# GpSimd's row transfers issued singly, weight splits in pairs, and the tail of attention in another order

## The chip, the core and the metric

The kernel runs on one core of one Trainium2 chip. The metric is the device time of the whole launch in microseconds (us). Five engines work side by side and in order, each on its own list of instructions: TensorE (PE; its weight loads are shown as PEld), VectorE (DVE), ScalarE (ACT), GpSimd (POOL) and SyncE (SP), which issues most transfers. They wait for one another through semaphores.

## The reference

The program is an attention layer whose output rows go through a mixture of eight experts. Cut to what is computed:

```python
# attention: 4 batches, 8 heads, 768 positions, head size 64
scores = q @ k.T / sqrt(64) + bias            # bias falls with distance, one slope per head
keep   = first 8 positions, or the 96 positions up to the row's own
a      = softmax(where(keep, scores, -1e9));  x = (a @ v), rows of 512 for 3072 tokens
# experts: 8, one per token
logits = x @ w_gate + modality_bias[modality_id]
e      = argmax(logits);  gate = softmax(logits)[e]
out[t] = gate[t] * (relu(x[t] @ w1[e]) @ w2[e])      # w1 512x1024, w2 1024x512
```

## The kernel before

**Attention.** The 3072 tokens are 24 blocks of 128 rows. `step(n)` (one per block, software pipelined) puts on TensorE the scores of block n (L235), the transposes of the probabilities of block n-1 (`pt`, L279), the product with the values of block n-2 (`pv`, L301 and L313), and the router's small products of blocks n-3 and n-4 (`gate_a`, `gate_b`, `gate_c`: `tx`, `lp`, `lq`). `xr` scales a finished block and stores its rows to `x_rows`. One batch is six blocks; after each batch `route_a` to `route_f` find every token's expert and its place in a sorted list, and `route_c` writes six times 128 entries of that list (`ids_sorted`) by an indirect transfer from GpSimd.

**Experts.** Tokens of one expert are worked off in slots, in this order: e0, e1 (512 rows each, from the first two batches), p0 (512), g0 (128), p1 (512), g1 (128), p2 (512), u0 (256). A slot of 512 rows has eight groups, one of 128 has two, and one of 256 four. A group is `l1` (twelve matmuls into `ph`; ReLU on ScalarE gives `hh`, VectorE gives the remainder `hl`) and, one group later, `l2` through `finish_group` (twelve matmuls into `po`). Every operand is split into a high and a low part, so each product takes three matmuls. Such names carry the slot: `php` and `pop` are those of a p slot, `phg` and `pog` of a g slot; `ahp`/`alp` and `bhp`/`blp` are the two parts of a p slot's first and second weights. A g slot has tokens on the other side, and transposes its hidden rows (`l1_t`).

**What a slot needs beforehand.** Its weights are loaded by SyncE in eight pieces of 512 KB into six buffers `raw`; a buffer is loaded again once its piece has been split. `split` does one piece: ScalarE rounds it (L606), VectorE subtracts (L607). Its rows are fetched from `x_rows` by GpSimd (`gather_x`, 128 rows a transfer, tile `xg`), and `x_t` transposes one such tile on TensorE (`mt`) and splits it on ScalarE and VectorE (`xh`, `xl`). The results go out by GpSimd, 128 rows a transfer (`fin`, L775). A single set of up to 32 leftover tokens (`few_x`, `few_t`, `few_l1`, `few_ht`, `few_l2`) is worked in plain fp32 beside e1 and p0; `few_l2` (L738) is 64 small matmuls straight from the raw weights.

**The order.** The order on TensorE, ScalarE and VectorE is the order in which the code is written (`manual_schedule`). In the loop over slots u and groups g, `run(k)` takes k splits from a sorted list of due ones, and `fill` issues writes and gathers and transposes the next slot's rows. GpSimd and SyncE have queues that are placed by the framework's own simulation and worked in order. `spaced(ins, x)` makes an instruction wait for instruction x.

Of the kernel before, what the change touches and what calls it, by code (L numbers as in the profile page):

```python
# [19 lines left out]
P = 128  # L20
# [6 lines left out]
NBLK = NT // P  # L27
# [37 lines left out]
def moe_attention_kernel(  # L65
# [278 lines left out]
    def gate_a(b, i):  # L344
        xv = xrs.pop((b, i))
        tx = p_t(f"tx{b}_{i}")
        for c in range(4):
            nc.tensor.transpose(tx[:, c * P : (c + 1) * P], xv[:, c * P : (c + 1) * P], ident)
# [61 lines left out]
    by = [pv_end]  # L410

# [40 lines left out]
    def route_c(b, j):  # L452
# [8 lines left out]
        if b + 1 < B:  # L461
            spaced(ins, by[0])
# [105 lines left out]
    def gather_x(s, ts, early=False):  # L568
        if 0 in ts:
            s.xg = xgp.tile([P, 4, DM], F32, tag="xg", name=f"xg{s.name}")  # L570
        for t in ts:
            ins = nc.gpsimd.indirect_dma_start(
                out=s.xg[:, t, :],
                out_offset=None,
                in_=s.xsrc,
                in_offset=bass.IndirectOffsetOnAxis(ap=s.ui[:, t, 0:1], axis=0),
            )
            if early:
                spaced(ins, pv_end)
            elif s.straight:  # L580
                spaced(ins, pe_end)
# [110 lines left out]
    def few_x(s):  # L692
        s.xg = mp.tile([M, DM], F32, tag="xgf", name="xgf")
        nc.gpsimd.indirect_dma_start(
# [4 lines left out]
        )  # L699

# [377 lines left out]
    for b in range(B):  # L1078
# [8 lines left out]
        for j in range(NB):  # L1087
            at(n0 + NB + 7 + (j // 3 if b else j), route_c, b, j)
# [95 lines left out]
    for u in range(2):  # L1184
        at(LAST + 4 + u, lambda u=u: gather_x(eslots[0], (2 * u, 2 * u + 1), True))
# [90 lines left out]
    e0.mx = mx[0]  # L1276
    x_t(e0, 0)
# [16 lines left out]
    gate_c(*gates(NBLK - 2))  # L1294
# [6 lines left out]
    def rest():  # L1301
        by[0] = pe_end
        late = [job for n in sorted(todo) for job in todo[n]]
        writes.extend(args for f, args in late if f is route_c)
        for f, args in late:
            if f is route_c:
# [113 lines left out]
    def fill(u, g):  # L1420
# [5 lines left out]
        for i in range(2):  # L1426
            if writes and (writes[0][0], "pi") in rt:
                route_c(*writes.pop(0))
        if len(order) == NE and len(slist) == NPS + NUS + NGR and not writes:

            order.extend(slist[j] for j in ORDER)
            load_on()
# [10 lines left out]
        if nx is not None:  # L1443
            nx.mx = mx[(u + 1) % 2]
            if s.nt == 4 and 3 <= g < 3 + nx.nt:
                x_t(nx, g - 3)
            elif s.nt < 4 and 2 * g + 1 < nx.nt:
                x_t(nx, 2 * g + 1)
# [159 lines left out]
```

## Time and profile before

| | before |
|---|---|
| runs shown | 465.87, 467.57, 471.68 us; median 467.57 |
| profiled execution | 465.37 us, span 463.6 us |
| TensorE | busy 432.3 us, 93% of the span; mean granted clock 0.986 |
| VectorE, ScalarE, GpSimd | 57%, 50%, 25% |
| chain that ended last | PE 82%, issue 7%, ACT 6%, DVE 3%, POOL 1% |

Attention lasts until about 140 us, then comes a tail in which the last blocks' router products and the first slot's row transposes share TensorE, and from about 156 us on the expert slots follow each other. The last row of the table is the chain of waits followed back from the end; "issue" in it is time in which the engine waited for nothing that the profile shows.

### The profile page before, as it was taken

How to read it: one execution, taken by the hardware profiler on the slowest of the kernel's cores; microseconds unless marked ns; L12 is line 12 of the kernel's file. 1: busy time of each engine (PE TensorE's matmuls, PEld its weight loads, DVE VectorE, ACT ScalarE, POOL GpSimd, SP SyncE). 2: the span in 40 equal slices, each digit the busy share in tenths (PEclk: the TensorE clock that was granted, in tenths of full speed). 3: DMA queues.
4: the chain of work that ended last, by engine and by line, in shares of the span. 5: the costliest groups of instructions: out<-in, count | busy, mean ns of one | idle time of the engine just before them, and what ended most of it. 6: DMA issues, size and time to landing. Idle time of an engine off the chain costs nothing.

```text
span 463.6 us, 11673 instructions
## 1 busy us (share of the span) xinstructions
PE 432.3 (93%) x4376; PEld 357.8 (77%) x4376; DVE 266.2 (57%) x892; ACT 232.6 (50%) x635; POOL 114.8 (25%) x243
## 2 busy tenths in 40 slices
PE   7999999999898896999999979998999987999994
PEld 6888888887777684788887758886888865888993
DVE  7887888787795473878543313356333455343540
ACT  6887788787774331435332413266333464232631
POOL 7500031157642077003500520004500050000031
PEclk9999999999998999999999989999999998999998
DMA  8999999999887152235612362248732485323121
GB/s 285 349 329 349 348 357 350 325 333 281 301 283 306 69 178 82 85 119 185 212 46 93 105 219 90 95 153 298 240 129 90 135 258 197 123 93 103 65 91 52
DMA packets 37873, 90.44 MB, mean 195 GB/s; under 512 B 6047, under 2 KB 8095, under 8 KB 37808
## 3 DMA queue, kind: packets, MB, share of 16 engines
q1 hardware_dynamic: 32848, 76.29, 49.4%
q0 software_dynamic: 4672, 12.85, 7.9%
q8 instruction: 36, 0.59, 0.6%
q10 hardware_dynamic: 288, 0.48, 0.3%
q14 instruction: 29, 0.24, 0.2%
HBM read 75.21 MB, written 14.45 MB: 193 GB/s over the span
## 4 chain that ended last, share of the span: by engine, by line
PE 82%; issue 7%; ACT 6%; DVE 3%; POOL 1%; POOLq 0%; ACTq 0%; DVEq 0%
PE pt L279 8%; PE s L235 6%; PE x L313 5%; PE php L654 5%; PE php L652 5%; PE php L653 5%; PE pop L680 4%; PE pop L681 4%; PE pop L682 4%; PE phe L652 3%; PE poe L680 3%; PE poe L682 3%; PE poe L681 3%; PE phe L654 3%; PE phe L653 3%
## 5 line engine op out<-in xcount | busy, mean ns | idle before, releaser
L265 ACT ACTIVATE pr<-sc,nmx 128x168 f32<-128x168 f32 x192 | 81.0, 424 | 20.2 <-DVE nmx L254 20.2
L656 DVE SCALAR_TENSOR_TENSOR hlp<-php,hhp 128x512 fp32r<-128x512 f32 x24 | 16.6, 692 | 81.4 <-ACT hhp L655 78.1
L254 DVE CUSTOM_DVE_ANT_0 sc<-s,tbl 128x168 f32<-128x168 f32 x192 | 50.8, 328 | 7.7 <-PE s L235 7.5
L655 ACT ACTIVATE hhp<-php 128x512 fp32r<-128x512 f32 x24 | 14.4, 598 | 78.3 <-PE php L654 78.3
L279 PE MATMUL pt<-ident,pr 128*128 128x128 f32 x288 | 45.7, 289 | 1.6 <-DVE rin L325 0.5
L288 DVE COPY pT<-pt 128x384 f32<-128x384 f32 x72 | 37.7, 549 | 15.4 <-PE pt L279 12.7
L652 PE MATMUL php<-xhp,ahp 128*128 128x512 f32 x96 | 39.2, 408 | 4.3 <-ACT ahp L606 4.3
L279 PEld LDWEIGHTS pt<-ident,pr 128*128 128x128 f32 x288 | 30.8, 143 | 13.4 <-issue 5.3
L235 PE MATMUL s<-kt,qt 64*64 64x168 f32 x768 | 38.2, 319 | 3.0 <-DVE lgt L367 1.8
L654 PE MATMUL php<-xhp,alp 128*128 128x512 f32 x96 | 38.5, 401 | 1.2 <-DVE alp L607 1.2
L653 PE MATMUL php<-xlp,ahp 128*128 128x512 f32 x96 | 38.1, 397 | 0.0
L680 PE MATMUL pop<-bhp,hhp 128*128 128x512 f32 x96 | 37.6, 391 | 0.0
L682 PE MATMUL pop<-bhp,hlp 128*128 128x512 f32 x96 | 37.4, 390 | 0.0
L681 PE MATMUL pop<-blp,hhp 128*128 128x512 f32 x96 | 37.4, 389 | 0.0
L455 POOL DMA_INDIRECT ids_sorted<-tki,pi x24 | 24.6, 1025 | 50.7 <-PE lq L366 20.1
L265 ACT ACTIVATION_READ_ACCUMULATOR pr<-sc,nmx 128x1 f32 x192 | 36.1, 188 | 0.0
L235 PEld LDWEIGHTS s<-kt,qt 64*64 64x64 f32 x768 | 27.7, 136 | 7.6 <-DVE lgt L367 2.4
L655 ACT ACTIVATE hhe<-phe 128x512 fp32r<-128x512 f32 x16 | 9.6, 598 | 46.5 <-PE phe L654 46.5
L313 PE MATMUL x<-vx,pT 128*64 128x64 f32 x768 | 28.8, 226 | 1.6 <-issue 1.5
L313 PEld LDWEIGHTS x<-vx,pT 128*64 128x64 f32 x768 | 25.0, 138 | 3.7 <-issue 2.0
L680 PE MATMUL poe<-bhe,hhe 128*128 128x512 f32 x64 | 25.1, 393 | 2.5 <-issue 2.5
L652 PE MATMUL phe<-xhe,ahe 128*128 128x512 f32 x64 | 26.0, 407 | 0.0
(378 smaller groups left out, 977.4 us busy)
## 6 DMA issues: line engine op xcount, KB each, us to landing
vx<-in_v_l SPq DMA_DIRECT2D x24, 512.0 KB
kt<-in_k_t SPq DMA_DIRECT2D x23, 464.0 KB
x_rows<-xr SPq DMA_DIRECT2D x24, 256.0 KB
qt<-in_q_t SPq DMA_DIRECT2D x23, 256.0 KB
vl<-in_v_s SPq DMA_DIRECT2D x48, 96.0 KB
rawe0a<-in_moe_w SPq DMA_DIRECT2D x4, 512.0 KB
rawe0b<-in_w SPq DMA_DIRECT2D x4, 512.0 KB
rawe1a<-in_moe_w SPq DMA_DIRECT2D x4, 512.0 KB
```

The lines of the kernel that those rows point to most:

```text
L235: nc.tensor.matmul(ps[h][64 * half : 64 * half + 64, c : c + W], qt[hs, hp, 64 * half : 64 * half + 64], kt[hs, hp, k0 : k0 + W], start=Tr ...
L254: V.tensor_tensor_reduce(out=sc, in0=pss[n, hp // 2][h][:, hp % 2 * W : (hp % 2 + 1) * W], in1=(tbl0 if n % NB == 0 else tbl)[:, hh, :], o ...
L265: last[0] = nc.scalar.activation(pr[:, h * (PRW - W) : h * (PRW - W) + W], sc, AF.Exp, bias=nmx[:, hh : hh + 1], scale=-1.0, accum_out=sum ...
L279: nc.tensor.transpose(tp[:, j * P : (j + 1) * P], pr[:, o : o + P], ident)
L288: V.tensor_copy(pT.rearrange("p a b -> p (a b)"), tp[:, 0 : 3 * P])
L313: pv_end[0] = nc.tensor.matmul(px[h][64 * half : 64 * half + 64, hp * D : (hp + 1) * D], pT[:, 2 * h, 64 * half : 64 * half + 64], vx[:, h ...
L652: nc.tensor.matmul(out_, hi, xh, start=(c == 0), stop=False)
L653: nc.tensor.matmul(out_, hi, xl, start=False, stop=False)
L654: pe_end[0] = nc.tensor.matmul(out_, lo, xh, start=False, stop=(c == 3))
L680: nc.tensor.matmul(s.po[t], hh[:, tt], hi, start=(fc == 0), stop=False)
L681: nc.tensor.matmul(s.po[t], hh[:, tt], lo, start=False, stop=False)
L682: pe_end[0] = nc.tensor.matmul(s.po[t], hl[:, tt], hi, start=False, stop=(fc == 7))
```

## The change

GpSimd's transfers: in attention, the list entries of batches two to four are written two per step instead of three, one step earlier, and within a step (as the early gathers of e0) they wait in turn for the last value product and for the last `gate_a` transpose. In the slots, `fill` only puts gathers in a list, and a new function `move` issues one gather or one write after `l1` and one after `l2`, each held until the latest matmul there; before, a whole slot's gathers were issued together, and the last batch's writes waited for no matmul.

Splits: `run` takes two per group in slots of 512 rows from e1 on (before one). In a g slot the next slot's first weights are split first, and its rows are transposed two tiles before each `l2` (before one before and one after). Tail: two router products are placed ahead of e0's transposes.

```diff
+        by[0] = tx_end if b and j % 2 else pv_end       # write_in_step(b, j), then route_c(b, j)
...
-        if b + 1 < B:
+        if (by[0] or [None])[0] is not None:
             spaced(ins, by[0])
...
-            at(n0 + NB + 7 + (j // 3 if b else j), route_c, b, j)
+            at(n0 + NB + 6 + (j // 2 if b else j), write_in_step, b, j)
...
-    for u in range(2):
-        at(LAST + 4 + u, lambda u=u: gather_x(eslots[0], (2 * u, 2 * u + 1), True))
+    for t in range(4):
+        at(LAST + 4 + t // 2, lambda t=t: gather_x(eslots[0], t, tx_end if t % 2 else pv_end))
...
+    gate_b(*gates(NBLK - 3))
+    gate_a(*gates(NBLK - 2))
     x_t(e0, 0)
     x_t(e0, 1)
     rinv(NBLK - 1)
     pv(NBLK - 1)
     sQ.close()
     mp = pool("mp")
-    gate_b(*gates(NBLK - 3))
-    gate_a(*gates(NBLK - 2))
     gate_c(*gates(NBLK - 3))
+    xr(NBLK - 1)
+    gate_b(*gates(NBLK - 2))
     x_t(e0, 2)
-    xr(NBLK - 1)
     x_t(e0, 3)
     gate_a(*gates(NBLK - 1))
-    gate_b(*gates(NBLK - 2))
+    gate_c(*gates(NBLK - 2))
...
-        for i in range(2):
-            if writes and (writes[0][0], "pi") in rt:
-                route_c(*writes.pop(0))
...
-            gather_x(order[ahead[1]], range(order[ahead[1]].nt))
+            s2 = order[ahead[1]]
+            gathers.extend((gather_x, s2, t) for t in range(s2.nt))
             if ahead[1] == NE:
-                few_x(fs[0])
+                gathers.append((few_x, fs[0]))
...
+    def move():
+        if gathers:
+            f, *args = gathers.pop(0)
+            if f is gather_x:
+                args.append(pe_end)
+            f(*args)
+        elif writes and (writes[0][0], "pi") in rt:
+            route_c(*writes.pop(0))
...
-            to_small = g + 1 == s.groups and nx is not None and nx.nt < 4
             if u or g:
-                run(2 if to_small or s.nt == 2 else 1 if s.nt == 4 else 2 * (1 - g))
-            if s.nt < 4 and nx is not None and 2 * g < nx.nt:
-                nx.mx = mx[(u + 1) % 2]
-                x_t(nx, 2 * g)
+                run((2 if u else 1) if s.nt > 1 else 2 * (1 - g))
+                move()
+            if s.nt < 4 and nx is not None:
+                for t in range(2 * g, min(2 * g + 2, nx.nt)):
+                    next_rows(u, t)
             if before:
                 finish_group(*before)
...
             if s.nt == 1 and g == 0:
                 run(2)
+            if not u or 0 < g < 7:
+                move()
             fill(u, g)
```

How instructions move is not to be read from those lines alone, so three places follow, each with the list of one engine before and after.

**ScalarE, the turn from g0 to p1, before.** `hrg`/`hhg` are g0's hidden rows, `xhp<-mtp` the rows of p1, `ahp<-rawp1a` p1's first weights, `hhp` the first group of p1.

```order
L664 CAST hhg_5233<-phg_5232 128x512
L606 CAST bhg_5310<-rawg0b_5133 128x1024
L606 CAST bhg_5316<-rawg0b_5168 128x1024
L618 CAST xhp_5261<-mtp_5335 128x4x128
L641 ACTIVATE hrg_5357<-phg_5342 128x512
L618 CAST xhp_5261<-mtp_5359 128x4x128
L664 CAST hhg_5343<-phg_5342 128x512
L618 CAST xhp_5261<-mtp_5385 128x4x128
L606 CAST ahp_5392<-rawp1a_5212 128x1024
L606 CAST ahp_5398<-rawp1a_5218 128x1024
L655 ACTIVATE hhp_5405<-php_5404 128x512
```

The same list after the change, from g0's first group on:

```order
L645 ACTIVATE hrg_5259<-phg_5244 128x512
L610 CAST ahp_5261<-rawp1a_5154 128x1024
L610 CAST ahp_5265<-rawp1a_5160 128x1024
L622 CAST xhp_5269<-mtp_5271 128x4x128
L622 CAST xhp_5269<-mtp_5278 128x4x128
L779 ACTIVATE obp_5290<-pop_4936,uip_4524 128x512
L779 ACTIVATE obp_5298<-pop_4937,uip_4524 128x512
L779 ACTIVATE obp_5306<-pop_4938,uip_4524 128x512
L779 ACTIVATE obp_5314<-pop_4939,uip_4524 128x512
L668 CAST hhg_5245<-phg_5244 128x512
L610 CAST bhg_5325<-rawg0b_5066 128x1024
L610 CAST bhg_5331<-rawg0b_5072 128x1024
```

Before, the two casts of p1's first weights are the last thing ahead of p1's first group. Now they stand ahead of p0's four results (`obp`), a whole group earlier. The turn from g1 to p2 moves in the same way, and there a second split of g1's own first weights also leaves the turn.

**GpSimd, e0's slot, before, with what each instruction waits for** (`DMASW` is an older transfer of its own, `PE` a matmul).

```order
L572 DMA xge_3951<-x_rows,uie_3347 128x512 [waits DMASW4_49]
L572 DMA xge_3951<-x_rows,uie_3347 128x512 [waits DMASW5_49]
L455 DMA ids_sorted<-tki,pi_3652 25088x16 [waits DMASW6_49,PE_49]
L455 DMA ids_sorted<-tki,pi_3652 25088x16 [waits DMASW7_49]
L455 DMA ids_sorted<-tki,pi_3652 25088x16 [waits DMASW0_49,PE_49]
L455 DMA ids_sorted<-tki,pi_3652 25088x16 [waits DMASW1_49]
L455 DMA ids_sorted<-tki,pi_4038 25088x16 [waits DMASW2_49,DVE_49]
L455 DMA ids_sorted<-tki,pi_4038 25088x16 [waits DMASW3_49]
```

The same place after:

```order
L577 DMA xge_3958<-x_rows,uie_3347 128x512 [waits DMASW5_49,PE_49]
L577 DMA xge_3958<-x_rows,uie_3347 128x512 [waits DMASW6_49,PE_49]
L461 DMA ids_sorted<-tki,pi_3652 25088x16 [waits DMASW7_49,PE_49]
L461 DMA ids_sorted<-tki,pi_3652 25088x16 [waits DMASW0_49,PE_49]
L461 DMA ids_sorted<-tki,pi_3652 25088x16 [waits DMASW1_49,PE_49]
L461 DMA ids_sorted<-tki,pi_4037 25088x16 [waits DMASW2_49,DVE_49,PE_49]
L461 DMA ids_sorted<-tki,pi_4037 25088x16 [waits DMASW3_49,PE_49]
```

The order is the same but for one write that has gone ahead of the gathers; what is new is that each transfer waits for a matmul of its own. The same wait stands at the gathers of the later slots.

**TensorE, the tail of attention, before** (`mte` are e0's rows, `phe` its first group).

```order
L357 MATMUL lp_3_3803<-xT_3_3723,cst 32x128 x4
L348 MATMUL tx_4_3810<-ident,xr_3714 128x128 x4
L366 MATMUL lq_3_3817<-sel,lps_3_3808 128x8
L615 MATMUL mte_3820<-ident,xge_3503 128x128 x4
L615 MATMUL mte_3831<-ident,xge_3503 128x128 x4
L348 MATMUL tx_5_3838<-ident,xr_3827 128x128 x4
L357 MATMUL lp_4_3845<-xT_4_3815,cst 32x128 x4
L652 MATMUL phe_3856<-xhe_3745,ahe_3176 128x512
```

After, behind the last value products:

```order
L366 MATMUL lq_3_3819<-sel,lps_3_3752 128x8
L357 MATMUL lp_4_3826<-xT_4_3759,cst 32x128 x4
L619 MATMUL mte_3833<-ident,xge_3503 128x128 x4
L619 MATMUL mte_3840<-ident,xge_3503 128x128 x4
L348 MATMUL tx_5_3847<-ident,xr_3822 128x128 x4
L366 MATMUL lq_4_3854<-sel,lps_4_3831 128x8
L656 MATMUL phe_3861<-xhe_3761,ahe_3176 128x512
```

`lp_3` and `tx_4` have gone ahead of e0's first two row transposes, and `lp_4` ahead of the other two; on VectorE the last block's `xr` now comes ahead of the second pair of `xl`, not between them.

## Rows read from the trace of the kernel before

**Rows 1.** Page, parts 1 and 3: busy time; an instruction queue's packets and MB.

```profile
PE 432.3 (93%) x4376; PEld 357.8 (77%) x4376; DVE 266.2 (57%) x892; ACT 232.6 (50%) x635; POOL 114.8 (25%) x243
...
q8 instruction: 36, 0.59, 0.6%
```

**Rows 2.** Waits of PE: line waited for, us in total, times, longest.

```profile
PE php L652 <- ACT ahp L606: 4.3, 2, 2.6
...
PE s L235 <- DVE lgt L367: 1.8, 2, 1.2
PE tx L348 <- DVE xr L334: 1.6, 1, 1.6
PE phg L636 <- ACT ahg L606: 1.3, 1, 1.3
PE php L654 <- DVE alp L607: 1.2, 2, 0.7
...
PE phg L637 <- DVE alg L607: 0.8, 1, 0.8
```

**Rows 3.** ScalarE in order of time at the first turn: start, us, line, operation.

```profile
319.74 2.00 ACT L606 CAST ahp<-rawp1a 128x1024 fp32r<-128x1024 f32 x2
```

**Rows 4.** SyncE's queue in order of time, same stretch.

```profile
305.67 1.52 SPq L589 DMA_DIRECT2D rawp1a<-in_moe_w  x2
```

**Rows 5.** Stretches: length, busy (instructions) by engine, PE clock, DMA share, GB/s.

```profile
270.20:273.00 2.80, 2.80 (x20) 2.12 (x20) 0.00 (x0) 0.37 (x1) 0.99 (x1) 0.50 0.89 306
386.30:389.00 2.70, 2.67 (x6) 2.15 (x7) 1.11 (x1) 0.00 (x0) 0.00 (x0) 0.50 0.88 285
210.00:220.00 10.00, 10.00 (x45) 8.26 (x44) 8.87 (x27) 4.52 (x7) 4.28 (x4) 1.00 0.64 215
```

**Rows 6.** TensorE in order of time around the write burst.

```profile
179.15 0.39 PE L654 MATMUL phe<-xhe,ale 128*128 128x512 f32 x1
...
187.05 0.60 PE L615 MATMUL mte<-ident,xge 128*128 128x128 f32 x4
```

**Rows 7.** GpSimd in order of time: writes, results, gathers.

```profile
171.04 1.00 POOL L455 DMA_INDIRECT ids_sorted<-tki,pi  x1 [0.30 <-issue]
...
182.58 1.51 POOL L455 DMA_INDIRECT ids_sorted<-tki,pi  x1 [0.31 <-issue]
210.14 1.27 POOL L775 DMA_INDIRECT out<-obe,oie  x1 [26.05 <-ACT obe L774]
...
226.92 0.89 POOL L694 DMA_INDIRECT xgf<-x_rows,uif  x1 [0.31 <-issue]
...
258.70 1.02 POOL L775 DMA_INDIRECT out<-obe,oie  x1 [29.62 <-ACT obe L774]
...
268.03 1.01 POOL L775 DMA_INDIRECT out<-obe,oie  x1 [0.30 <-issue]
```

**Rows 8.** TensorE in order of time at the few tokens' second layer.

```profile
264.03 1.39 PE L738 MATMUL pof<-rawp0b,hTf 128*32 128x128 f32 x37
...
270.20 1.13 PE L738 MATMUL pof<-rawp0b,hTf 128*32 128x128 f32 x16 [1.03 <-issue]
271.26 0.80 PE L652 MATMUL php<-xhp,ahp 128*128 128x512 f32 x1
```

**Rows 9.** Stretches, one attention step each; columns as in Rows 5.

```profile
102.34:107.75 5.41, 5.41 (x123) 4.78 (x122) 4.55 (x25) 4.50 (x19) 4.48 (x14) 1.00 1.02 323
113.55:120.49 6.94, 6.18 (x123) 4.93 (x122) 4.80 (x25) 4.81 (x20) 4.80 (x12) 1.00 0.96 327
120.49:127.67 7.18, 5.96 (x124) 5.00 (x123) 5.41 (x27) 5.21 (x21) 4.94 (x18) 1.00 0.81 269
```

**Rows 10.** GpSimd in order of time in those steps, first and last write.

```profile
118.24 1.07 POOL L455 DMA_INDIRECT ids_sorted<-tki,pi  x1 [1.04 <-PE x L313]
...
120.88 0.96 POOL L455 DMA_INDIRECT ids_sorted<-tki,pi  x1 [0.30 <-issue]
```

**Rows 11.** TensorE in order of time: the few tokens' rows transposed.

```profile
232.61 0.43 PE L704 MATMUL mtf<-ident,xgf 32*128 32x32 f32 x4
```

More of the change, by code (lines that the diff above doesn't have):

```diff
@@ L410, in moe_attention_kernel, with write_in_step @@
     by = [pv_end]
+    tx_end = [None]
+    def write_in_step(b, j):
+        by[0] = tx_end if b and j % 2 else pv_end
+        route_c(b, j)
     def route_b(b):
@@ L566, in ld_x, with gather_x @@
         nc.sync.dma_start(s.ui[:, 0 : s.nt, :], ids[ds(so, n), :].rearrange("(p t) o -> p t o", t=s.nt))
-    def gather_x(s, ts, early=False):
-        if 0 in ts:
+    def gather_x(s, t, by=None):
+        if t == 0:
             s.xg = xgp.tile([P, 4, DM], F32, tag="xg", name=f"xg{s.name}")
[L571 to L581, printed above, removed]
+        ins = nc.gpsimd.indirect_dma_start(
+            out=s.xg[:, t, :],
+            out_offset=None,
+            in_=s.xsrc,
+            in_offset=bass.IndirectOffsetOnAxis(ap=s.ui[:, t, 0:1], axis=0),
+        )
+        if by is not None:
+            spaced(ins, by)
+        s.got = t + 1
     def ld_w(s, which, h, j):
@@ L699, in few_x @@
         )
+        spaced(ins, pe_end)
     def few_t(s):
@@ L1303, in rest @@
         late = [job for n in sorted(todo) for job in todo[n]]
-        writes.extend(args for f, args in late if f is route_c)
+        writes.extend(args for f, args in late if f is write_in_step)
         for f, args in late:
-            if f is route_c:
+            if f is write_in_step:
                 continue
@@ L1425, in fill @@
             next(bg, None)
-        for i in range(2):
-            if writes and (writes[0][0], "pi") in rt:
-                route_c(*writes.pop(0))
         if len(order) == NE and len(slist) == NPS + NUS + NGR and not writes:
             order.extend(slist[j] for j in ORDER)
+            nx = order[u + 1]
             load_on()
@@ L1438, in fill, with next_rows @@
         if ahead[1] < min(ahead[0], u + 3):
-            gather_x(order[ahead[1]], range(order[ahead[1]].nt))
+            s2 = order[ahead[1]]
+            gathers.extend((gather_x, s2, t) for t in range(s2.nt))
             if ahead[1] == NE:
-                few_x(fs[0])
+                gathers.append((few_x, fs[0]))
             ahead[1] += 1
-        if nx is not None:
-            nx.mx = mx[(u + 1) % 2]
[L1445 to L1448, printed above, removed]
+        if nx is not None and s.nt == 4 and 3 <= g < 3 + nx.nt:
+            next_rows(u, g - 3)
+    gathers = []
+    def move():
[6 more added lines that the diff above has]
+            route_c(*writes.pop(0))
+    def next_rows(u, t):
+        nx = order[u + 1]
+        nx.mx = mx[(u + 1) % 2]
+        assert nx.got > t
+        x_t(nx, t)
     next(bg)
@@ L1524, in leftover @@
                     ld_w(s, *part)
-                gather_x(s, (0,))
+                gather_x(s, 0)
                 x_t(s, 0)
```

6 lines of the change are left out of this document (2 added, 4 removed).

## The prediction

> **What bounds the kernel now.** I read the busy times first. TensorE is busy for 432.3 us of 463.6 [rows 1], so it is the bound, and a change can only win where TensorE stands idle or runs at the low clock. I then looked at the span in stretches of 10 us and found the idle time in few places: the last attention steps, the tail before e0, one place in e0, one at the few tokens' second layer, the two turns from a g slot to a p slot, and the drain at the end. The waits of TensorE name what ended part of it [rows 2]: at a p slot's first product the split weights, 4.3 us on ScalarE and 1.2 us on VectorE in two turns; in the second turn g1's own splits, 1.3 and 0.8 us; in the tail 1.6 us for `xr`. Other gaps have no releaser ("issue"). For those I laid TensorE and GpSimd side by side in order of time. Ten list writes go out one after another from 171.04 to 184.1 us [rows 7]; TensorE ends a group at 179.15 and comes to the next slot's transposes only at 187.05 [rows 6]. Eight results and gathers go out from 258.70 to 269.0 [rows 7]; the 64 matmuls of `few_l2` fall apart from 265 on, with a gap of 1.03 us before the last sixteen [rows 8]. In two attention steps with three writes each [rows 10] the step takes 6.94 and 7.18 us, where one without such a burst takes 5.41 [rows 9].
>
> **The change part by part.** It adds and removes no matmul, split or transfer; everything is moved.
>
> *The two turns.* In the first, ScalarE starts the two casts of p1's first weights at 319.74 [rows 3], when TensorE has nothing else. Now they stand a group earlier, under two `l1` and two `l2` of twelve matmuls: at 45 matmuls in 10.0 us [rows 5], 0.22 us each, that is 10.7 us of cover against 2.0 us of casts. The waits 4.3 + 1.2 + 1.3 + 0.8 = 7.6 us end. After the second turn TensorE runs from 386.30 to 389.00 at clock 0.50, which is 1.2 GHz, after having been idle for most of 4 us; half of 2.7 us, 1.35, comes back if the idle goes. Together 8.95. What is late next is the last row tile: its cast and subtraction follow g0's two second-weight splits on ScalarE and VectorE. Between 0 and 2.6 us, the longest such wait now [rows 2], I take 0.4 a turn, near the low end, because one tile's parts are a fraction of the two casts waited for now. Gain 8.1, bounds 3.8 (twice 2.6 left) and 8.95.
>
> *Writes in e0's slot.* Twelve matmuls at 0.22 us are 2.7; from 179.38 to 187.05 are 7.7 us, so 4.9 are lost [rows 6]. Now the ten writes are a half group apart, from about 162 to 198, and the last four of them end later than now. Who waits for them: the list reads of p0, which stand on SyncE's queue behind a weight load; p0's gathers come at e1's third group, ten groups of 5.4 us after e0's first at 156 us and so near 212 us or later, and p0's first transposes a group and a half behind. At least 14 us lie between the last write and that gather, so the delay costs nothing; without this cover it would cost up to 14 us, by which the last write comes later. I take 4.4 of the 4.9, bounds 0 and 4.9.
>
> *Gathers of p1.* The 64 matmuls of `few_l2` take from 264.03 to 271.26, 7.2 us; at the rate of the first 37, 1.39 us, they need 2.4; then the low clock, 0.50 from 270.20 to 273.00 [rows 5], costs half of the remaining 1.74 us. Lost: 4.8 + 0.9 = 5.7 [rows 8]. Now the four results go first and only two gathers fall before and into `few_l2`, not four; but the results stay in a row, and the weight loads for g0 start at the same place as before. I take half, 2.8, bounds 0 and 5.7.
>
> *Attention steps.* 6.94 + 7.18 - 2 x 5.41 = 3.3 us above a plain step [rows 9]; two writes a step, each held by a matmul, in place of three; e0's first splits stay in the second step. I take half, 1.6, bounds 0 and 3.3.
>
> *Tail.* `xr` is no longer behind a split, so TensorE's 1.6 us before `tx` go [rows 2]; what is late next is the last tile's subtraction. I take 1.4, bounds 0 and 1.6.
>
> *New wait.* The gather of the few tokens' rows is now issued after e1's fifth `l1`, and `few_t` stands right behind the `l2` that follows: 2.7 us. Its issue alone takes 0.89 us [rows 7]; before, transposes came 5.69 us after it [rows 11] and did not wait. So the wait is between 0 and 3.0; I take 0.5, near the low end, since it moves only 32 rows. All other gathers have at least three half groups. Behind held transfers on GpSimd stand results, whose four buffers are wanted again only a slot later.
>
> Costed at nothing: two splits in one group. ScalarE's 2.0 us of casts [rows 3] and VectorE's subtractions fit under a group's 5.4 us of matmuls; without that they would hold the next ReLU.
>
> **Sum.** 8.1 + 4.4 + 2.8 + 1.6 + 1.4 - 0.5 = 17.8 us. The profiled execution took 465.37, so 447.6. The median shown is 2.2 higher; I say 448.
>
> **Rival 1: the gaps without a releaser are not the bursts' doing.** For it: from 210.14 on four results go out in a row, and from 210 to 220 TensorE runs 45 matmuls in 10.00 us without a gap [rows 5, 7]. Against it: three places, each with gaps that begin inside a burst and end within 3 us of it. Then the e0, `few_l2` and step terms stay: 465.4 - 8.1 - 1.4 + 0.5 = 456.4.
>
> The trace lists one queue of 36 instruction packets with 0.59 MB, 16 KB each [rows 1], so TensorE's program does come through the transfer engines. The Trainium skill, "Runtime: NRT & Kernel Launch", section "Instruction fetch mechanics", says that each sequencer fetches such blocks over a queue of its own while it works off the one before, and that the cost of crossing a block is mostly hidden. By that rule GpSimd's bursts would not stop TensorE's program, which is this rival; the size of the packets agrees, the gaps inside the bursts speak against "hidden".
>
> **Rival 2: data late in place of splits late.** p1's first weights were issued at 305.67 [rows 4] and used 14.1 us later [rows 3], which is all that is known of their landing. Now the load comes one group, 5.4 us, earlier and the use 10.7 us earlier, which leaves 8.8. If landing takes more than that, ScalarE stands before the results of p0 and the turn waits again. At the worst, 5.3 us a turn, the turns win nothing: 465.4 - 9.7 = 455.7. Against it: a piece of 512 KB, at the 215 to 306 GB/s of [rows 5], moves in about 2.4 us or less once its turn has come.
>
> **Rival 3: slower.** 31 transfers in the slots become single and tied to TensorE. If each stops TensorE for a gap, the bursts' 4.9 + 5.7 us go, but a gap of about 1.03 us [rows 8] comes with each: 456.4 - 10.6 + 31 x 1.03 = 477.7. It decides from 0.63 us a transfer on. Against it: the same 10 us without a gap.
>
> **Chances and range.** Forecast 0.60 (443 to 452); rival 1 0.20 (454 to 459); rival 2 0.10 (453 to 459); rival 3 0.04; 0.06 that nearly all of 24.5 us is won, near 441. The range that holds eight in ten is 442 to 457.5. About 2% is what a measurement of this kernel tells from no change; 2% below the median is 458.2, above most of rivals 1 and 2. Faster 0.84, within 0.12, slower 0.04.
>
> **What would show it.** Right: no wait of `php` on `ahp` or `alp` over 0.7 us; e0's slot without a gap over 1 us; `few_l2` under 5 us; steps with writes under 6.5 us; `tx` without a wait for `xr`; a wait of `few_t`'s transposes under 1 us. Wrong: gaps of about 1 us beside single transfers (rival 3), gaps where no transfer runs (rival 1), or ScalarE waiting for a transfer at `ahp` (rival 2).

## The result and the profile after

| | before | after |
|---|---|---|
| median, runs of this comparison | 469.51 us (465.87 to 471.68) | 448.24 us (448.03 to 449.7) |
| profiled execution, span | 465.37, 463.6 us | 448.08, 446.4 us |
| mean granted clock | 0.986 | 0.993 |

The ratio is 0.9561, interval 0.9486 to 0.9636: faster. Forecast were 448 us and a sum of 17.8 us; the profiled executions differ by 17.3, the medians by 21.3, since before's profiled execution is shorter than each of its four runs. Ratios, here and below, are of fast runs alone: on the chip of e9 to e11 five of before's eleven runs are slow, and its median is 454.23 us with them and 451.3 without. The sum hides errors of both signs, so the span is cut where TensorE begins a group (first and last rows of the named products):

| stretch of TensorE, us | before | after | gain |
|---|---|---|---|
| A: to e0's first product | 155.73 | 155.67 | 0.1 |
| B: e0's first product to e1's last | 102.93 | 102.69 | 0.2 |
| C: to g0's first transposes | 24.46 | 18.76 | 5.7 |
| D: to u0's first transposes | 125.99 | 115.37 | 10.6 |
| E: to the last product | 48.09 | 48.10 | 0.0 |
| behind it, to the end of the span | 6.4 | 5.8 | 0.6 |

The page after, busy time, answers to [rows 1]: as many matmuls, 4.7 us less of busy time, at a shorter span.

```profile
PE 427.6 (96%) x4376; PEld 356.9 (80%) x4376; DVE 264.1 (59%) x892; ACT 233.8 (52%) x635; POOL 115.0 (26%) x243
```

Waits of TensorE after the change (line waited for, us in total, times, longest) answer to [rows 2]. The waits for `ahp`, `alp`, `ahg`, `alg` and `xr` are gone; one is new, `mtp` for `xgp`, and most of the rest is idle time without a releaser in the attention steps.

```profile
PE x L313 <- issue: 4.4, 9, 1.2
PE mtp L619 <- DMA xgp<-x_rows,uip: 2.3, 1, 2.3
```

TensorE after, in order of time (start, us, line, operation), answers to [rows 8, 11]: the few tokens' rows are transposed without a wait, `few_l2` takes 2.29 us, and at the first turn p1's product follows the transposes of g0's hidden rows in 0.36 us.

```profile
232.32 0.40 PE L709 MATMUL mtf<-ident,xgf 32*128 32x32 f32 x4
...
263.73 2.29 PE L743 MATMUL pof<-rawp0b,hTf 128*32 128x128 f32 x64
...
312.55 0.60 PE L667 MATMUL phg<-ident,hrg 128*128 128x128 f32 x4
312.91 0.48 PE L656 MATMUL php<-xhp,ahp 128*128 128x512 f32 x1
```

Stretches of TensorE after (length, busy with count, clock, DMA share, GB/s) answer to [rows 5, 9]: the two turns run without a gap at full clock. The two steps with the first writes take 7.63 and 6.25 us; only the second is under the 6.5 that I had named. At p0's first product the clock is 0.58.

```profile
109.76:117.39 7.63, 6.25 (x123) 1.00 0.77 247
117.39:123.64 6.25, 5.84 (x124) 1.00 0.84 270
224.80:228.20 3.40, 3.40 (x12) 0.58 0.55 161
310.00:320.00 10.00, 10.00 (x47) 1.00 0.84 290
370.00:380.00 10.00, 10.00 (x47) 1.00 0.97 338
```

**The new wait.** Three engines after the change, each in order of time. SyncE's queue first: the five issues of p0's weights that come before the read of p0's row list (`uip`).

```profile
200.50 5.82 SPq L593 DMA_DIRECT2D rawp0a<-in_moe_w  x2
207.07 5.05 SPq L598 DMA_DIRECT2D rawp0b<-in_w  x2
212.91 0.38 SPq L593 DMA_DIRECT2D rawp0a<-in_moe_w  x1
213.74 0.33 SPq L572 DMA_DIRECT2D uip<-ids_sorted  x1
```

GpSimd: the gather that needs the list (idle time before it and what ended it in brackets).

```profile
220.49 0.99 POOL L577 DMA_INDIRECT xgp<-x_rows,uip  x1 [7.89 <-DMA uig<-ids_sorted]
```

TensorE: the transposes that need the gathered rows.

```profile
221.73 0.39 PE L686 MATMUL poe<-bhe,hle 128*128 128x512 f32 x1
224.47 0.63 PE L619 MATMUL mtp<-ident,xgp 128*128 128x128 f32 x4 [2.35 <-DMA xgp<-x_rows,uip]
```

The list is read at 213.74, and the gather goes out at 220.49; in e1 below, whose only change is the place of this read, it goes out at 213.90. (The bracket names g0's list, `uig`, the last to land by the profile; in e1 the gather goes out before `uig` is even read, so it is p0's that it needs.) TensorE stands 2.35 us and then works for 3.4 us at a low clock.

### The profile page after: what moved, and what is told of

It reads as the page before. It is cut to its first block, busy times and chain, and to the rows that moved or that the text cites. A ratio compares the mean times of both kernels' runs of the same rounds, so it can differ in the third digit from the quotient of the medians.

```text
span 446.4 us, 11699 instructions
## 1 busy us (share of the span) xinstructions
PE 427.6 (96%) x4376; PEld 356.9 (80%) x4376; DVE 264.1 (59%) x892; ACT 233.8 (52%) x635; POOL 115.0 (26%) x243
## 4 chain that ended last, share of the span: by engine, by line
PE 81%; issue 5%; DVE 5%; DMA 3%; ACT 2%; SPq 1%; POOL 1%; POOLq 0%
PE pt L279 7%; PE s L235 6%; PE x L313 5%; PE php L656 5%; PE php L657 5%; PE php L658 5%; PE pop L686 5%; PE pop L685 5%; PE pop L684 5%; PE phe L657 3%; PE phe L656 3%; PE phe L658 3%; PE poe L684 3%; PE poe L686 3%; PE poe L685 3%
## 5 line engine op out<-in xcount | busy, mean ns | idle before, releaser
L780 POOL DMA_INDIRECT out<-obp,oip x12 | 13.9, 1162 | 114.1 <-ACT obp L779 111.7
L279 PEld LDWEIGHTS pt<-ident,pr 128*128 128x128 f32 x288 | 30.2, 141 | 13.8 <-DVE pT L288 6.4
L656 PE MATMUL php<-xhp,ahp 128*128 128x512 f32 x96 | 38.2, 398 | 0.0
L235 PE MATMUL s<-kt,qt 64*64 64x168 f32 x768 | 36.3, 318 | 1.4 <-DVE nmx L254 1.1
L658 PE MATMUL php<-xhp,alp 128*128 128x512 f32 x96 | 37.4, 390 | 0.0
L313 PE MATMUL x<-vx,pT 128*64 128x64 f32 x768 | 30.5, 226 | 5.1 <-issue 4.4
```

What stands on the lines that cost most here:

```text
L235: nc.tensor.matmul(ps[h][64 * half : 64 * half + 64, c : c + W], qt[hs, hp, 64 * half : 64 * half + 64], kt[hs, hp, k0 : k0 + W], start=Tr ...
L279: nc.tensor.transpose(tp[:, j * P : (j + 1) * P], pr[:, o : o + P], ident)
L313: pv_end[0] = nc.tensor.matmul(px[h][64 * half : 64 * half + 64, hp * D : (hp + 1) * D], pT[:, 2 * h, 64 * half : 64 * half + 64], vx[:, h ...
L656: nc.tensor.matmul(out_, hi, xh, start=(c == 0), stop=False)
L658: pe_end[0] = nc.tensor.matmul(out_, lo, xh, start=False, stop=(c == 3))
```

## The experiments

Each series of up to four kernels ran on a chip of its own, with the kernel before beside it: 470.42, 470.09, 454.23 and 453.21 us there (medians of runs 1 to 4, 5 to 8, 9 to 11, and 12). Times are to be compared within a series only. The intervals of e3 and of e9 to e11 reach across a ratio of 0.98, so these four are not told from a change of 2%. The stretches of TensorE in the traces, cut as above:

| kernel | median | ratio to before, interval | B | C | D |
|---|---|---|---|---|---|
| after | 448.24 | 0.9561 [0.9486, 0.9636] | 102.69 | 18.76 | 115.37 |
| e1_read_first | 445.48 | 0.9483 [0.9438, 0.9528] | 98.64 | 19.63 | 115.39 |
| e2_burst_writes | 445.61 | 0.9477 [0.9416, 0.9538] | 98.49 | 19.38 | 115.38 |
| e3_late_splits | 458.79 | 0.9770 [0.9707, 0.9832] | 98.54 | 20.46 | 129.12 |
| e4_extra_writes | 445.71 | 0.9489 [0.9432, 0.9545] | 98.58 | 19.61 | 115.39 |
| e5_before_again | 466.73, one run | | 104.06 | 25.62 | 127.62 |
| e6_turns_only | 454.79 | 0.9676 [0.9628, 0.9725] | 109.65 | 18.27 | 115.37 |
| e7_burst_gathers | 443.29 | 0.9423 [0.9380, 0.9467] | 98.51 | 18.37 | 115.42 |
| e8_writes_later | 447.23 | 0.9504 [0.9461, 0.9546] | 98.62 | 19.32 | 115.40 |
| e9_extra_eighteen | 440.07 | 0.9780 [0.9694, 0.9865] | 98.27 | 18.27 | 115.46 |
| e10_quiet_tail | 439.68 | 0.9751 [0.9682, 0.9821] | 99.88 | 18.27 | 115.39 |
| e11_alternate | 442.37 | 0.9817 [0.9754, 0.9879] | 99.03 | 18.26 | 115.44 |
| e12_before_extra | 452.23 | 0.9984 [0.9948, 1.0019] | 97.99 | 18.27 | 127.84 |

**e1_read_first**: after, with p0's list read put on SyncE's queue ahead of p0's weights.

```diff
+            ld_x(order[NE])                # ahead of the loads of p0's weights
...
-            ld_x(order[ahead[0]])
...
+            else:
+                ld_x(order[ahead[0]])
```

> The changed kernel, with one line moved: the read of p0's list is issued ahead of the weight loads that become due at the same place, not behind them. Theory (the list read stood on SyncE's queue, and in the transfer engines, behind five weight loads, and its landing held p0's gathers from 213.96 to 220.49 us): the read goes out near 200 us, the four gathers go out one per half group at about 214, 217, 219.5 and 222, TensorE's 2.35 us wait at p0's first transposes and the 1.6 us at half clock behind it disappear, in all about 4.2 us: near 444 us. Rival A (the wait is that of the first gather's own hold, three half groups are too short for four gathers and their landing): the gathers still end too late, 448 us. Rival B (the weight loads, now one read later, come too late for the casts of p0's first weights at 219.9 us): the wait moves to ScalarE, 447 to 450 us.

SyncE's queue in e1, in order of time:

```profile
199.84 0.33 SPq L572 DMA_DIRECT2D uip<-ids_sorted  x1
200.43 5.55 SPq L593 DMA_DIRECT2D rawp0a<-in_moe_w  x2
```

GpSimd in e1: the gather now waits for its matmul, not for the list.

```profile
213.90 0.99 POOL L577 DMA_INDIRECT xgp<-x_rows,uip  x1 [1.62 <-PE phe L658]
```

TensorE has no wait before p0's transposes, at 221.62. B falls by 4.05 us. The list read, and nothing else, was the new wait. (e1's time alone, 2.8 us lower on another chip, would not show it: the intervals overlap.)

**e2_burst_writes**: e1, with e1's gathers and e0's writes issued in a row again, as before.

```diff
-            if (by[0] or [None])[0] is not None:
+            if b + 1 < B and (by[0] or [None])[0] is not None:
...
+        for i in range(2):
+            if writes and (writes[0][0], "pi") in rt:
+                route_c(*writes.pop(0))
```

> As the kernel of the first run of this series (p0's list read first), but e1's gathers and e0's list writes go out as before the change: two writes per filled place, the gathers together, the last six writes without a hold, so that some ten transfers follow each other on GpSimd. Theory (a run of some ten GpSimd transfers makes TensorE's instructions come late, with no releaser): a stretch of 4 to 5 us is lost in e0 between about 175 and 190 us, and the time is 4 to 5 us above that of the first run, since nothing behind absorbs it now. Rival (the lost stretch of before had another cause, for example where a block of TensorE's program ended): e0's slot stays without a gap and the time equals that of the first run within 1 us.

Fourteen transfers went out from 165.00 to 184.35, and TensorE did not stop (stretch of TensorE in e2):

```profile
160.00:200.00 40.00, 40.00 (x193) 1.00 0.38 125
```

But ScalarE stood still beside them. In e2, in order of time, its cast of row tiles and the ReLU behind it:

```profile
182.64 0.59 ACT L622 CAST xhe<-mte 128x512 fp32r<-128x512 f32 x1 [4.23 <-PE phe L658]
185.59 0.60 ACT L659 ACTIVATE hhe<-phe 128x512 fp32r<-128x512 f32 x1 [2.36 <-PE mte L619]
```

The same cast in e1:

```profile
182.70 0.59 ACT L622 CAST xhe<-mte 128x512 fp32r<-128x512 f32 x1 [1.56 <-PE mte L619]
```

In e1 the cast starts 0.64 us after its transposes began on TensorE (182.06), in e2 4.05 us after (178.59). ScalarE is 3.4 us late in e2, and TensorE's lead of a group swallows it. That a burst beside long matmuls always stops TensorE has fallen; a burst does hold an engine up here. Time and B are those of e1, as the rival said, on a chip where before takes 470.42 (no trace of before is from there).

**e3_late_splits**: after, with the splits and row tiles placed as before.

```diff
-                run((2 if u else 1) if s.nt > 1 else 2 * (1 - g))
+                to_small = g + 1 == s.groups and nx is not None and nx.nt < 4
+                run(2 if to_small or s.nt == 2 else 1 if s.nt == 4 else 2 * (1 - g))
```

> The changed kernel, with the splits and the next slot's row tiles placed as before the change (one split a group, two only ahead of a small slot, one row tile a group in g slots); GpSimd's transfers and the tail stay as changed. Theory (the two turns from a g slot to a p slot were the largest term): the waits for the split weights come back, 7.6 us, and with them the low clock behind the second turn; from the traces of before and after, 2.7 us are lost at the first turn and 7.9 at the second, 10.6 in all: near 459 us. Rival (part of that was won by the gathers and loads that start at other times): 4 to 7 us, 452 to 455 us.

The waits of TensorE in e3 show those of before again, number by number:

```profile
PE php L656 <- ACT ahp L610: 4.3, 2, 2.6
...
PE phg L640 <- ACT ahg L610: 1.3, 1, 1.3
PE php L658 <- DVE alp L611: 1.2, 2, 0.7
...
PE phg L641 <- DVE alg L611: 0.8, 1, 0.8
```

D is 13.7 us longer than in e1, the time 13.3. And p0's list read, in after's place in the program, comes at 211.93 behind three loads, not five; its gather waits for a matmul, and B is 98.54. So the split edit brings both the gain at the turns and the new wait.

**e4_extra_writes**: e1, with ten more list writes in a row in p1's slot and ten more, a half group apart, in p2's.

```diff
+                if u == 4 and g == 5:
+                    for w in range(10):
+                        more(0, w, pe_end)
+                if u == 6 and 2 <= g < 7:
+                    more(1, 2 * (g - 2), pe_end)
```

> As the first run of this series, with twenty additional list writes of 128 rows of 64 bytes to two tables that nobody reads: ten in a row on GpSimd in p1's slot, from its sixth group on, where nothing else goes out (about 335 us), and ten in p2's slot, one per half group, each held by TensorE. Theory (it is the run of transfers that stops TensorE): a stretch of 3 to 6 us is lost in p1's slot, beginning some 6 to 8 us after the first of the ten and ending within 3 us of the last; nothing is lost in p2's slot. First rival (any GpSimd transfer costs TensorE a gap of 0.4 to 1 us): 4 to 10 us are lost in each of the two slots. Second rival (not the transfers): both slots stay at full busy time and the time is that of the first run.

Neither kind cost anything (TensorE in the two stretches of e4); the time is that of e1. Rival 3, a gap with each single transfer, is dead.

```profile
341.50:355.80 14.30, 14.30 (x64) 1.00 0.25 79
380.00:410.00 30.00, 30.00 (x138) 1.00 0.26 85
```

**e5_before_again**: the kernel before, for one more trace on the second chip.

> The kernel before, unchanged, for a second trace of it. Theory (the lost stretches in e0 and at the few tokens' second layer belong to this order of transfers): they come back at the same places and sizes, 4.9 us and 4.8 us, within 1 us each. Rival (they are accidents of one execution): at least one of the two is absent or under half its size.

The gaps of [rows 6, 8] are there again: in e0 at 178.33 to 183.29 (0.65, 0.90, 0.32, 0.31 us and less; 4.6 us lost by the prediction's reckoning), and `few_l2` from 263.30 to 270.19, 6.9 us (4.5 lost). They belong to the kernel on this chip, not to one execution.

**e6_turns_only**: before, with the split and row edit alone.

```diff
-                run(2 if to_small or s.nt == 2 else 1 if s.nt == 4 else 2 * (1 - g))
+                run((2 if u else 1) if s.nt > 1 else 2 * (1 - g))
...
-                x_t(nx, 2 * g)
+                for t in range(2 * g, min(2 * g + 2, nx.nt)):
+                    x_t(nx, t)
```

> The kernel before, with only the splits and row tiles at the turns as changed (two splits a group, row tiles of a g slot two in its first group); GpSimd's transfers and the tail as before. Theory (the turns are worth 10.6 us by the two traces): 10 to 11 us below the kernel before, a ratio of 0.977, and no wait on ahp, alp, ahg or alg. What then stays to the changed kernel, about 6.7 us, are the few tokens' second layer (5.7) and e0's stretch (4.6) less the new wait at p0's rows (4.3). Rival (the turns owe a part to the transfers' new places): 5 to 8 us below.

The time fell by 15.3 us, more than theory or rival had: besides D, which is after's, C falls. No wait on `ahp`, `alp`, `ahg` or `alg` is left. B is the longest of all, 109.65: e0's gaps are there, and p0's list comes late here too; GpSimd and TensorE in e6, in order of time:

```profile
230.14 0.99 POOL L572 DMA_INDIRECT xgp<-x_rows,uip  x1 [7.67 <-DMA uig<-ids_sorted]
```

```profile
186.48 0.40 PE L680 MATMUL poe<-bhe,hhe 128*128 128x512 f32 x1 [1.38 <-issue]
...
273.41 1.95 PE L738 MATMUL pof<-rawp0b,hTf 128*32 128x128 f32 x64
```

e0's gaps stay where the writes stay in a row. But `few_l2` takes 1.95 us although its results and gathers are still in a row, at 267.32 to 278.33. C falls by 6.2 us with the split edit alone, and by 4.0 with all the rest (e3): either brings most of after's 5.7. What differs is where `few_l2` lies against the transfers. In before and e5 four of them begin between 0.2 us ahead of it and 4.0 us into it (7.2 and 6.9 us long), in e3 two (4.1), in after, e1, e6, e7 and e8 one, 1.3 to 1.4 us into it (2.0 to 3.3). A longer `few_l2` also takes in more of them, and e6 and e7 lose nothing with their one, so that the transfers' places are the cause is argued, not shown.

**e7_burst_gathers**: e1, with p1's gathers issued together as before.

```diff
+            if ahead[1] == 4:
+                for t in range(s2.nt):
+                    gather_x(s2, t, pe_end)
```

> As the first run of this series, but p1's four gathers go out together, as before the change, among e1's four results, instead of one per half group. Theory (the run of eight transfers there makes TensorE's instructions come late just where they are shortest, in the 64 small matmuls of the few tokens' second layer): these matmuls take 5 to 7.5 us in place of about 3, and the time is 3 to 5.5 us above the first run. Rival (as the extra writes in p1's slot showed, a run of transfers does no harm of itself; before the change it was something else): the matmuls stay under 3.5 us and the time equals the first run's within 1 us.

My theory that these gathers in a row stretch `few_l2` fell; C is even 0.95 us shorter than with the single gathers of e8 on the same chip (TensorE in e7, its transfers 1.3 us apart):

```profile
260.23 1.95 PE L743 MATMUL pof<-rawp0b,hTf 128*32 128x128 f32 x64
```

This version's 443.29 us is the best on a chip where before takes 470; its interval lies below after's.

**e8_writes_later**: e1, with the second batch's writes one step later and held by another matmul.

```diff
-            at(n0 + NB + 6 + (j // 2 if b else j), write_in_step, b, j)
+            at(n0 + NB + 6 + (j // 2 + (b == 1) if b else j), write_in_step, b, j)
```

> As the first run of this series, but the second batch's six list writes, two a step, go out one step later and are held by the step's last weight transposes, not by its value products. Theory (in the attention steps, where TensorE's instructions are shortest, a pair of writes makes them come late): the three gaps of 0.47 us in the value products near 112 us and the one of 0.4 us near 118 disappear, and gaps of the same size stand 1 to 3 us behind the new places of the pairs, in the scores and the first value products; the time changes by less than 2 us. Rival (the gaps belong to the place in TensorE's program): they stay where they were, near 112 and 118 us.

The gaps moved with the writes. GpSimd and TensorE in e8, in order of time:

```profile
115.88 1.11 POOL L462 DMA_INDIRECT ids_sorted<-tki,pi  x1 [4.72 <-PE lq L366]
117.29 0.97 POOL L462 DMA_INDIRECT ids_sorted<-tki,pi  x1 [0.30 <-issue]
```

```profile
117.84 0.29 PE L301 MATMUL x<-vl,pT 40*64 40x64 f32 x2 [0.43 <-issue]
118.62 0.51 PE L301 MATMUL x<-vl,pT 40*64 40x64 f32 x15 [0.49 <-issue]
```

The pairs at 122.99 and 130.16 are followed by such gaps at 125.03 and 132.16. In a step of short matmuls a pair of writes does stop TensorE, on this chip: the two gaps behind it make 0.8 to 0.9 us, and the three steps with pairs take 7.12 to 7.16 us where the step ahead of them takes 5.48.

**e9_extra_eighteen**: e7, with four more writes before e1's results and eighteen in a row in p1's slot.

```diff
+                if u == 4 and g == 4:
+                    for w in range(18):
+                        more(w, pe_end)
```

> As the seventh run (p0's list read first, p1's gathers together), with 22 additional list writes to tables that nobody reads: four in a row on GpSimd ahead of e1's results, so that the transfers behind them slide into the few tokens' second layer, and eighteen in a row in p1's slot from its fifth group on. Theory for the first place (each transfer that begins while TensorE works through the 64 small matmuls costs it about 1.3 us; in the traces so far none cost nothing, one 1.0 to 2.2, four 4.9 to 5.3): the matmuls take 4 to 6 us in place of 1.95. Rival: they stay under 2.5 us. Theory for the second place (ten in a row did no harm in p1's slot because a run has to last over some 10 to 14 us before ScalarE falls behind, as in e0, where ScalarE stood for 6.8 us within a run of sixteen): with eighteen, 23 us long, one ReLU at least comes over 2 us late, and TensorE loses 1 to 5 us there. Rival (it is not the length, but what else the engines do there; in e0 VectorE plans and SyncE loads): ScalarE stays on time and TensorE without a gap. The total is 0 to 10 us above the seventh run.

Both rivals came. In the first place `few_l2` takes 1.95 us with a transfer that begins 0.26 us into it; the forecast's reading of the traces, a cost for each such transfer, had left out that e6 and e7 have one and take 1.95 as well. No gap beside the eighteen (TensorE is busy for 23.60 of 23.60 us from 328.40 on), and ScalarE kept its time. But on this chip the first pair of writes, at 110.27 and 111.62, makes no gap either, so this says nothing on how long a burst must be.

**e10_quiet_tail**: e7, with the two writes in the tail moved into e0's slot.

```diff
+            at(n0 + NB + 6 + (j // 2 + (b == 2) if b else j), write_in_step, b, j)
```

> As the seventh run, but the two list writes that the change puts into the tail, among the last block's value products, go out in e0's slot like the ten others. Theory (these two cost TensorE two gaps of 0.3 to 0.4 us and what lies around them, and ate up the tail's own gain): both gaps near 152 us disappear and TensorE reaches e0's first product 0.8 to 1.6 us sooner after the last scores, 442 us. Rival (the tail is bound by ScalarE and VectorE there): no change within 0.4 us, 443.3.

The same time as e9; the 442 and 443.3 of the forecast came from another chip. The gaps beside these writes that after shows at 151.81 and 152.54 were absent in e9 too, so nothing was there to win; untested on the other chips.

**e11_alternate**: e10, with GpSimd's planning work cut in halves between the second batch's writes.

```diff
+        for j in (2 * w, 2 * w + 1):
+            with tc.issue_after(plan_end[0].ins):
+                write_in_step(1, j)
+            plan_part()
```

> As the tenth run, but in the three attention steps with two writes each GpSimd's planning is cut into halves, and write and half plan alternate, so that no two writes follow each other at once (about 2.3 us apart instead of 1.3). Theory (only a second transfer close behind a first one makes TensorE's instructions late in these steps): the gaps near 112 and 118 us disappear, and the three steps take 5.5 to 5.9 us in place of 7.7, 6.2 and 6.3: 2 to 3 us less than the tenth run. Rival (every transfer in a dense stretch costs, near or far from the next): six gaps, of 0.4 us or more in all six places, and no gain or a loss of up to 1 us.

2.7 us slower than e10 by the medians, with ranges that overlap; no gaps were there to remove: e10's three steps take 5.48, 5.48 and 5.72 us.

**e12_before_extra**: before, with eighteen writes in a row in p1's slot.

```diff
+                if u == 4 and g == 4:
+                    for w in range(18):
+                        more(w, pe_end)
```

> The kernel before, with eighteen additional list writes in a row in p1's slot, from its fifth group on (tables that nobody reads). It has to tell two things apart. First: whether the stretches that the kernel before loses in e0 and at the few tokens' second layer go with the chip. Theory: where the kernel before takes about 470 us they are there (4 to 6 us and 4.5 to 5.5 us), where it takes about 452 us, as in the third series, they are absent (under 0.5 us each), and the difference of some 18 us is mostly these two, the attention steps and what else of TensorE's gaps has no releaser. Rival: at 452 us they are there as well, and the difference lies elsewhere. Second: on a chip with these stretches, whether a run of eighteen in p1's slot makes ScalarE late as the run of sixteen does in e0. Theory of length: a ReLU over 2 us late and a gap of 1 to 5 us on TensorE; rival (what else runs in e0): none. Total: as the kernel before, 0 to 5 us more.

This is the kernel before in all places of the argument, on a chip where before takes 453.21. Its sixteen transfers run in a row from 162.47 to 183.89, and four begin 0.22 us ahead of the start of `few_l2` and 1.38, 2.66 and 3.99 us behind it, to 0.02 us as in the trace of [rows 7, 8]. TensorE in e12, stretch and in order of time:

```profile
160.00:200.00 40.00, 40.00 (x188) 1.00 0.38 126
```

```profile
258.46 1.96 PE L738 MATMUL pof<-rawp0b,hTf 128*32 128x128 f32 x64
```

No gap in e0, none in `few_l2`; the two steps with the first three writes in a row take 5.48 us each, the next, behind the second three, 6.29, with a gap of 0.54 us at 126.99. The waits of TensorE in e12 keep those of the turns:

```profile
PE php L652 <- ACT ahp L606: 4.3, 2, 2.6
...
PE phg L636 <- ACT ahg L606: 1.3, 1, 1.3
```

So nearly all gaps without a releaser go with the chip, the waits of the turns with the kernel: B and C of the kernel before are 97.99 and 18.27 here, 102.93 and 24.46 in the trace that I predicted from. The forecast put the 18 us or so between the chips down mostly to these places; B, C and the three steps with writes (19.92 there, 17.25 here) make 13.8 us between the two traces, which differ by 10.0 as a whole, since D among others is longer in e12. How many transfers it takes on a chip that shows them stays open, as does after's own time on a chip like this one. Of its versions e9 to e11 gain 1.8 to 2.5% on a chip of that kind, where e7 gains 5.8% on the other.

## Why the prediction came out right, and what failed in it

**The step that failed** stands under the writes in e0's slot: "At least 14 us lie between the last write and that gather, so the delay costs nothing". I had counted the last write as the thing that the list reads wait for, and named the weight load ahead of them without counting how many. Two splits a group free the weight buffers earlier, so five loads, not three (e3), stood ahead of the read. It cost 4.3 us in B: 2.35 of standing, the rest low clock and the restart. e1 gives back 4.05.

**The turns** were said to bring 8.1, at most 8.95, and brought 10.6, which lies outside the bounds. The mechanism was right (e3, e6); the term was mis-sized. TensorE before, in order of time:

```profile
318.58 0.60 PE L615 MATMUL mtp<-ident,xgp 128*128 128x128 f32 x4
320.85 0.50 PE L652 MATMUL php<-xhp,ahp 128*128 128x512 f32 x1 [1.67 <-ACT ahp L606]
...
381.66 0.60 PE L615 MATMUL mtp<-ident,xgp 128*128 128x128 f32 x4
384.88 0.50 PE L652 MATMUL php<-xhp,ahp 128*128 128x512 f32 x1 [2.62 <-ACT ahp L606]
```

The idle time in brackets counts from the modelled end of the instruction before, 0.60 us after its start. Without a wait the next one starts 0.36 us after that start (312.55 to 312.91 in after). The wait of 1.67 thus costs 320.85 - 318.58 - 0.36 = 1.91 us. The six waits counted so make 8.8 in place of 7.6; the matmul after each takes 0.1 more to the next (0.33 for 0.23), 0.6 in all; the low clock is 1.4, as said. Together 10.8 against 10.6. Even so the size is that of one trace: D of the same kernel is 127.62 in e5 and 127.84 in e12, with the same waits, and so 12.2 and 12.4 us above the 115.4 of the changed kernels. The difference is the clock behind the first turn, TensorE in before and in e5 (length, busy with count, clock, DMA share, GB/s):

```profile
322.20:326.00 3.80, 3.80 (x17) 1.00 1.00 352
```

```profile
322.60:326.20 3.60, 3.60 (x10) 0.56 1.03 363
```

I had costed a low clock behind the second turn alone, since that trace has none behind the first. The 0.4 a turn "late next" did not come: TensorE has no wait in either turn.

**Writes in e0's slot**: said 4.4, measured 4.6, from e1's product ahead of p0's rows, which ends 226.74 before and 222.12 after. But the price was a chip's: e12 has the same writes and no gap. On the chip of the second series the gaps are there with the writes in a row (e5, e6) and not with single ones (e7, e8); but e2 has fourteen transfers in a row and no gap on another chip where before takes 470. That the spacing of the writes won these 4.6 us is likely, then, but not shown. Also the first 1.56 us of the gap behind [rows 6] was not TensorE's own. ScalarE before, in order of time, then TensorE:

```profile
180.45 0.60 ACT L655 ACTIVATE hhe<-phe 128x512 fp32r<-128x512 f32 x1 [10.71 <-PE phe L654]
```

```profile
181.10 0.50 PE L680 MATMUL poe<-bhe,hhe 128*128 128x512 f32 x1 [1.56 <-issue]
```

This ReLU's product ended at 173.61, and it starts 6.8 us later, 0.65 us before TensorE's matmul at 181.10 that needs it. ScalarE stood still first, beside the burst, as in e2; in e12, with the same burst, it did not.

**Gathers of p1**: said 2.8, measured 5.7 in C. I took half since half the gathers still fall there; all of the upper bound came. By e3 and e6 either edit alone brings most of it; with either, fewer transfers begin in `few_l2`, and beside the split edit the spacing of the gathers adds nothing (e7). In e12 the same four transfers cost nothing, so this price too was a chip's.

**Attention steps and tail**: said 1.6 + 1.4, measured 0.1 in A. The 3.3 us above a plain step were read as the writes' alone; but 1.8 of them are TensorE's waits for VectorE's `lgt` [rows 2], at 115.61 and 122.79, and the step that takes 7.18 us has one write in it, at 120.88, not three. The steps: GpSimd after, in order of time, answers to [rows 10], then TensorE in the same step.

```profile
111.18 1.05 POOL L461 DMA_INDIRECT ids_sorted<-tki,pi  x1 [2.97 <-PE s L235]
112.54 0.96 POOL L461 DMA_INDIRECT ids_sorted<-tki,pi  x1 [0.30 <-issue]
```

```profile
111.54 0.49 PE L313 MATMUL x<-vx,pT 128*64 128x64 f32 x7
112.49 0.25 PE L313 MATMUL x<-vx,pT 128*64 128x64 f32 x1 [0.46 <-issue]
113.20 0.29 PE L313 MATMUL x<-vx,pT 128*64 128x64 f32 x2 [0.46 <-issue]
113.94 0.90 PE L313 MATMUL x<-vx,pT 128*64 128x64 f32 x22 [0.46 <-issue]
```

The second write was to wait for a matmul of its own. By the time GpSimd comes to it that matmul is long done, so it goes out right behind the first, and gaps stay (7.63 us): the three steps with writes take 19.92 us before and 19.76 after. In the tail the 1.63 us for `xr` are gone, but two writes now stand in it, and TensorE has gaps of 0.39 and 0.38 us beside them. From the last step's scores to e0's first product it is 21.76 us before and 19.62 after, but 20.15 in e5 and 21.12 in e2, and A is 155.34 in e1 and 157.80 in e2, which are alike up to there: the tail's own share can't be told from one trace.

**The few tokens' rows**: said -0.5, measured 0, behind the wait at p0's rows; in e1 and e4, without that wait, 0.2.

The sum by its own terms: 10.6 + 4.6 + 5.7 + 0.1 - 4.3 + 0.6 (the drain, not foreseen) = 17.3. The errors, +2.5 + 0.2 + 2.9 - 2.9 + 0.5 - 4.3 + 0.6, nearly cancel: the total came out right by luck, its parts did not.

**The rivals.** Rival 2 is out: ScalarE never waits for a transfer at `ahp`. Rival 3 is out by e4. Rival 1 holds on two chips (e9 to e12, but for a gap of 0.5 to 0.8 us behind the last writes of attention in e9 and e12, and one as long some 7 us later, ahead of GpSimd's next transfer) and in the slots of long matmuls of e2 and e4; it does not hold in the attention steps on the chip of the second series, where the gaps moved with the writes (e8), and hardly in e0 on that chip, where gaps stand beside rows of writes (e5, e6) and not beside single ones (e7, e8). For e0 on the first series' chip e2 speaks for it. The rule of the Trainium skill, "Runtime: NRT & Kernel Launch", section "Instruction fetch mechanics", that the cost of crossing a block of instructions is mostly hidden, agrees with the runs without gaps. Where there are gaps, single matmuls come about 0.7 us apart (112.49, 113.20, 113.94 above), which is not hidden; but that these are fetches was only argued: of the traces' instruction packets none begins in that step's gaps or in those of before's e0, one in those of before's `few_l2` (265.58).

## What to carry to other kernels

When an edit frees buffers earlier, follow what that lets loose on the load queue: large loads go ahead of a small read that someone waits for, so issue the small read first (4 us here). A gap without a releaser is to be seen in a second trace, and if possible on another chip, before it is given a price. The waits with a releaser had the same length on every chip; measure them from start to start, with the restart and the low clock behind them, and take the clock from more than one trace, since it differed. Keep GpSimd's transfers out of dense stretches of short matmuls first (e8); between long ones twenty more, at most ten in a row, cost nothing in e4, while why before stops beside its sixteen on one chip and not on another is open.

## What the runs showed of the hardware

The same kernel takes 470 us on two chips and 453 to 454 on two others. Between the traces of before and e12 the difference shows where GpSimd's row transfers go out in a row (B 4.9, C 6.2, three attention steps 2.7 us). Where it shows, TensorE takes single matmuls some 0.7 us apart, with no releaser, and ScalarE stood still for 3.4 us (e2) and 6.8 us (before) with its input ready; TensorE did not stop for the first and did for the second. After waits of the same length at the first turn the granted clock stayed at 1.00 in before's trace and was 0.56 in e5's. By what path a transfer of GpSimd does that to other engines stays open.
